# Seven-product block method, first layer: sums of products continued in a PSUM bank, and some late sums moved from GpSimd to VectorE

## The chip, the cores and the metric

The kernel runs on one core of one Trainium2 chip. TensorE (PE in the profile) multiplies, with separate weight loads (PEld); VectorE (DVE), ScalarE (ACT) and GpSimd (POOL) work on elements; SyncE (SP) issues the transfers. The metric is the device time of one execution in microseconds (us). Everything is fp32 where this text is concerned.

## The reference

The program is an attention in which a query sees only keys of its own cluster, followed by a two-layer network with the activation h / (1 + exp(-1.702 h)).

```python
mask = q_assign[:, :, :, None] == k_assign[:, :, None, :]
scores = np.where(mask, scale * q @ k.T, -1e9)      # (4, 8, 768, 768)
x = (softmax(scores) @ v)                            # -> (3072, 512)
h = x @ w_in                                         # (512, 2048)
g = h * (1.0 / (1.0 + np.exp(-1.702 * h)))
return (g @ w_out).astype(np.float32)                # (2048, 512)
```

Four batches (b) of 768 tokens each go through it.

## The kernel before, in words

**Stages.** The attention of all four batches comes first. Batch 0's result stays in SBUF, that of batches 1 to 3 is stored to DRAM (`kept`, L580) and loaded again later. While the attention runs, VectorE also rounds the weights `w_in` and `w_out`. Then, batch by batch, come the first layer (`first7`, L847, once for each f from 0 to 7) and the second layer (`second49`, L890, once for each k from 0 to 6). The order of instructions on every engine is the order in which the Python code calls them; nothing is rescheduled.

**First layer.** A batch's x is cut into 2 x 2 blocks: X[c, h] has 256 of the 512 channels (half c) and 384 tokens (half h). `A_in(row, col, f)` is a piece of `w_in`: 128 outputs, piece f of half `row`, and channel half `col`. The four results of a turn f are `g1[:, 0]`, `g1[:, 1]` (output half 0, token halves 0 and 1) and `g2[:, 0]`, `g2[:, 1]` (output half 1), which are parts of the tile `G`. A plain product of 2 x 2 blocks takes eight block products; the kernel uses a block method with seven, whose operands are also sums of blocks: T1 to T4, sums of X blocks (`sums_x`, VectorE), and S1 to S4, sums of weight blocks (`sums_w`, L610, GpSimd, two turns ahead, in two rotating tiles `W`; S3 is made in place in `w_in`, in batch 0 only). Each block product is two matmul calls (two chunks of 128 channels) into one PSUM bank, and each call shows as two PE records. Seven products are A11·X, S2·T2, S1·T1, S3·T3, S4·X, A22·T4 and A12·X, in this order. Before, each takes a bank of its own out of six (`ps_b`), and VectorE puts them together in `G` with seven additions (`add`, L845); ScalarE copies the first product (L864) and applies the activation in place to the four results (`finish`, L859).

**After the first layer's turns.** `after7(f)` (L883) subtracts in `G` on VectorE, and from f = 4 on makes the first operands of the second layer (`sums_t`). In batch 0 the turns also carry the preparation of `w_out`: `sums_z` (turns 0 to 2, on GpSimd for every third f and on VectorE for the others), `turn_w` (turns 3 and 4, VectorE), and `keep_w` (turns 3 to 6, GpSimd: three sums, and a store of each to `kept_w` by SyncE).

**Second layer.** The same method on two levels: 7 x 7 = 49 products for each batch, seven in each call of `second49`. Already before, these go on in a bank with `start=False` while ScalarE copies the states. Its operands `temps(k)` (tiles E, Tx, Y, parts of G) are made by VectorE while the previous k runs (`extra`, L1087); its weights `Wz` are loaded from `kept_w`, except that in batch 0 the ones for k = 5 and 6 are made on the spot (`load_sums(k, made=True)`, L790). After each k the outer sums over `Y` run on GpSimd, in the last batch on VectorE for the blocks 5 and 7 (L941). In k = 5 and 6 VectorE also makes the next batch's T1 to T4.

**Memory reuse.** `att.close()` (L716) gives the attention's SBUF and PSUM back, and `G` lies there; the first instruction that writes `G`, ScalarE's copy of the first product of batch 0, therefore waits for everything that still used it, among others GpSimd and the stores of `kept`.

Of the kernel before, what the change touches and what calls it, by code (L numbers as in the profile page):

```python
# [8 lines left out]
FP32 = mybir.dt.float32  # L9
# [4 lines left out]
AF = mybir.ActivationFunctionType  # L14
# [24 lines left out]
def fast(  # L39
# [26 lines left out]
    nc = tc.nc  # L66

    B, H, S, D = q.shape
    NC = centroids.shape[1]
    DM, DF = moe_w_in.shape  # L70
    P = 128
    NJ = S // P
    HALF = S // 2
# [231 lines left out]
    for a in range(2):  # L305
        rows = slice(a * D, (a + 1) * D)
        nc.vector.tensor_copy(
            out=cT[rows, :, a, :],
# [287 lines left out]
    def sums(engine, todo):  # L596
        for o, a, op, b in todo:
            engine.tensor_tensor(out=o, in0=a, in1=b, op=(  # L598
                ALU.add if op == "+" else ALU.subtract))
# [3 lines left out]
    def A_in(row, col, f):  # L603

        at = (row * FB + f) * P
        return w_in[:, 2 * col:2 * col + 2, at:at + P]
# [164 lines left out]
        a = W_of(i)  # L771
        sums(nc.vector, ((a(0, 1), a(0, 0), "-", a(0, 1)),))

    def keep_w(k, o):

        a = W_of(ORDER[k])
        s2, s1, s4 = o
        for i, (o, x, op, z) in enumerate((
                (s2, a(1, 1), "-", a(0, 1)), (s1, s2, "+", a(0, 0)),
                (s4, a(1, 0), "-", s2))):  # L780
            sums(nc.gpsimd, ((o, x, op, z),))
            nc.sync.dma_start(out=kept_w[k, i], in_=o)

    def spare_y():
# [3 lines left out]
    W = {}  # L788

    def load_sums(k, made=False):  # L790
        W[k] = ws.tile([P, 3, FQ, P], FP32, name="Wz")
        if made:
            keep_w(k, [W[k][:, i] for i in range(3)])
            return
        for i in range(3):
            nc.sync.dma_start(out=W[k][:, i], in_=kept_w[k, i])
# [47 lines left out]
    def add(o, p, a):  # L844
        nc.vector.tensor_tensor(out=o, in0=p, in1=a, op=ALU.add)  # L845

    def first7(b, f, X, T):  # L847

        S = w_of.pop(b * FB + f)

        def product(a, x):
            ps = ps_b.tile([P, 512], FP32, name="b")
            for c in range(2):
                nc.tensor.matmul(out=ps[:, 0:HALF], lhsT=a[:, c], rhs=x(c),  # L854
                                 start=(c == 0), stop=(c == 1))
            return ps[:, 0:HALF]

        def finish(g):
            nc.scalar.activation(out=g, in_=g, func=AF.Gelu_apprx_sigmoid,  # L859
                                 scale=2.0)  # L860

        g1, g2 = G[:, f], G[:, f + FB]
        p = product(A_in(0, 0, f), lambda c: X[0, 0, c])
        nc.scalar.copy(g1[:, 0], p)  # L864
        p = product(S[2], lambda c: T[2, c])
        add(g2[:, 1], p, g1[:, 0])
        p = product(S[1], lambda c: T[1, c])
        add(g1[:, 1], p, g2[:, 1])
        p = product(S[3], lambda c: T[3, c])
        add(g2[:, 0], p, g2[:, 1])  # L870
        add(g2[:, 1], p, g1[:, 1])
        p = product(S[4], lambda c: X[1, 1, c])
        add(g1[:, 1], p, g1[:, 1])
        finish(g2[:, 1])
        p = product(A_in(1, 1, f), lambda c: T[4, c])
        add(g2[:, 0], p, g2[:, 0])
        finish(g1[:, 1])
        p = product(A_in(0, 1, f), lambda c: X[1, 0, c])
        add(g1[:, 0], p, g1[:, 0])
        finish(g2[:, 0])  # L880
        finish(g1[:, 0])

    def after7(f):  # L883

# [5 lines left out]
    def second49(k, extra, last):  # L890

        i = ORDER[k]
        a, g, t, w = W_of(i), G_of(i), temps(k), W.pop(k)
        A = {1: a(0, 0), 2: a(1, 0), 3: w[:, 2], 4: a(1, 1), 5: w[:, 1],
             6: w[:, 0], 7: a(0, 1)}
        M = {1: g(0, 0), 2: g(1, 0), 3: g(1, 1), 4: t[4], 5: t[1], 6: t[2],
             7: t[3]}

        def bank_b():
            return ps_b.tile([P, 512], FP32, name="b")[:, 0:QT]  # L900

        def product(ps, n, start):
            for f in range(FQ):
                nc.tensor.matmul(out=ps, lhsT=A[n][:, f], rhs=M[n][:, f],  # L904
                                 start=start and f == 0,
                                 stop=(f == FQ - 1), skip_group_check=True)

        y = Y[22] if i == 1 else ep.tile([P, 2, HALF], FP32, name="y")
        y11, y12, y21, y22 = (y[:, m, q * QT:(q + 1) * QT]
                              for m in range(2) for q in range(2))  # L910
        p5 = ep.tile([P, QT], FP32, name="p5")
        x = bank_b()
        product(x, 1, True)
        nc.scalar.copy(y11, x)
        z = bank_b()
        product(z, 2, True)
        add(y11, z, y11)
        extra(0)
        product(x, 6, False)
        nc.scalar.copy(y12, x)  # L920
        v = bank_b()
        product(v, 5, True)
        nc.scalar.copy(p5, v)
        product(x, 7, False)
        nc.scalar.copy(y22, x)
        add(y22, y22, p5)
        extra(1)
        product(v, 3, False)
        add(y12, v, y12)
        if i == 4:  # L930
            c = Y[21]
            add(c[:, 0], y[:, 0], c[:, 0])
            add(c[:, 1, QT:], y22, c[:, 1, QT:])
            extra(2)
        product(x, 4, False)
        if i == 4:
            add(c[:, 1, 0:QT], x, c[:, 1, 0:QT])
            return
        nc.scalar.copy(y21, x)
        extra(2)  # L940
        pool = nc.vector if last and i in (5, 7) else nc.gpsimd  # L941
        sums(pool, {1: (),
                    2: ((Y[11], y, "+", Y[22]),),
                    3: ((Y[12], y, "+", Y[22]),),
                    6: ((Y[12], y, "+", Y[12]), (Y[21], y, "+", Y[22])),
                    5: ((Y[12], y, "+", Y[12]), (Y[22], y, "+", Y[21])),
                    7: ((Y[22], y, "+", Y[22]), (Y[21], y, "+", Y[21]))}[i])
# [80 lines left out]
    for b in range(B):  # L1028
        for f in range(FB):
            first7(b, f, *XT)  # L1030
            sums_w(b * FB + f + 2)
            if f:
                after7(f - 1)
            do(pend, 1)
            if b == 0 and f < 3:
                for n in range(3 * f, min(3 * f + 3, FB)):
                    sums_z((nc.gpsimd, nc.vector, nc.vector)[n % 3], n)
            if b == 0 and f in (3, 4):
                for i in ORDER[0:4] if f == 3 else ORDER[4:]:
                    turn_w(i)  # L1040
            if b == 0 and f >= 3:
                for k in {3: (0,), 4: (1, 2), 5: (3,), 6: (4,), 7: ()}[f]:
                    keep_w(k, spare_y())
                if 5 <= f < 7:
                    load_sums(f - 5)
        after7(FB - 1)
        if b < B - 1:
            for h in range(2):
                for hp in range(HP):
                    x = xT_of[b + 1, h, hp] = xp.tile([P, HALF], FP32,  # L1050
                                                      name="x")
                    nc.sync.dma_start(out=x, in_=kept[b, h, hp])
            made = sums_x(b + 1)
        else:
            made = iter(())

        def stores(b, *todo, **how):
            for n in todo:
                store(b, n, **how)
                yield  # L1060

        def tail():
            store(b, 22)
            yield

        def chain(*todo):
            for steps in todo:
                yield from steps

        def sums_of_x():  # L1070
            for XT[:] in made:
                yield

        x_steps = sums_of_x()
        final = b == B - 1

        for k in range(7):
            nxt = sums_t(k + 1) if k < 6 else iter(())
            more = {1: sums_G(6), 2: sums_G(5), 3: sums_G(4),
                    4: stores(b, 11), 5: stores(b, 12) if final else x_steps,  # L1080
                    6: tail() if final else x_steps}.get(k, iter(()))
            if b == B - 1 and k < 2:
                test(k)
            if (b, k) == (B - 1, 6):
                is_bad = nc.values_load(bad[0:1, 0:1], min_val=0, max_val=1)

            def extra(at):  # L1087
                do(nxt, (2, 1, 1)[at])
                do(more, ((1, 0, 1) if final else (0, 4, 4))[at] if k == 6
                   else (0, 0, 4)[at] if k == 2 else (0, 2, 2)[at])  # L1090

            second49(k, extra, final)
            if k < 5:
                load_sums(k + 2, b == 0 and k > 2)
            elif b < B - 1:
                load_sums(k - 5)
        pend = () if final else stores(b, 12, 22, 21)
        if final:
            store_last(b)
# [439 lines left out]
```

## Time and profile before

| | us |
|---|---|
| median of 3 runs (lowest, highest) | 898.75 (898.56, 899.88) |
| the profiled execution: its time, its span | 900.34, 898.5 |
| PE busy | 885.8 (99%) |
| DVE busy | 728.3 (81%) |
| ACT busy | 366.1 (41%) |
| POOL busy | 497.4 (55%) |
| batch 0: first layer begins, second layer begins | 342.05, 414.33 |
| batch 1: first layer begins, second layer begins | 480.68, 554.83 |
| batch 2: first layer begins, second layer begins | 618.79, 691.03 |
| batch 3: first layer begins, second layer begins | 754.99, 827.23 |

The span runs from the first to the last instruction. Idle time before a group of instructions is put down to the releaser that came last. A line number such as L598 or L845 is that of a helper (`sums`, `add`), so the tile names tell the place. TensorE's granted clock was 0.999 of full speed.

### The profile page before, as it was taken

To read this page: it belongs to the slowest core of one execution; us is meant where nothing else is said; L and a number is where in the kernel's file an instruction comes from. 1 tells how busy PE (TensorE), PEld (TensorE's weight loads), DVE (VectorE), ACT (ScalarE), POOL (GpSimd) and SP (SyncE) were. 2 spreads that over 40 slices of the span, in tenths; PEclk is the share of its full clock that TensorE was granted. 3 is DMA by queue.
4 is the path that set the end of the run, shared out by engine and by line. 5 is a ranking of instruction groups with operands and counts; after the bars stand their busy time and mean duration, and the time that the engine had idled before them with its cause. 6 is when DMAs were issued, how large, how long until landed. Compare 5 with 4: busy or idle time off the path is not lost.

```text
span 898.5 us, 17781 instructions
## 1 busy us (share of the span) xinstructions
PE 885.8 (99%) x6720; PEld 581.4 (65%) x6720; DVE 728.3 (81%) x1183; ACT 366.1 (41%) x819; POOL 497.4 (55%) x469
## 2 busy tenths in 40 slices
PE   8999999999999999999999999999999999999997
PEld 3444444444444445558996557998556998556996
DVE  4999989999999997998998556798556798556795
ACT  3677767777677764322111232111232111222111
POOL 5899999998999998693274221143121134120130
PEclk9999999999999999999999999999999999999999
DMA  9566556666575310036113202223202223200224
GB/s 175 122 129 112 103 120 130 143 143 133 133 139 119 85 43 19 0 122 230 71 54 107 52 1 71 84 74 107 53 1 70 73 76 117 43 10 0 71 71 109
DMA packets 176333, 78.97 MB, mean 88 GB/s; under 512 B 152824, under 2 KB 159472, under 8 KB 176240
## 3 DMA queue, kind: packets, MB, share of 16 engines
q1 hardware_dynamic: 175984, 77.63, 35.2%
q8 instruction: 55, 0.90, 0.4%
q14 instruction: 38, 0.31, 0.1%
q10 hardware_dynamic: 256, 0.13, 0.1%
HBM read 61.03 MB, written 16.70 MB: 87 GB/s over the span
## 4 chain that ended last, share of the span: by engine, by line
PE 87%; DVE 8%; issue 2%; POOL 1%; DMA 1%; ACT 0%; SPq 0%; DVEq 0%; ACTq 0%; POOLq 0%
PE b L854 32%; PE b L904 23%; PE s L472 13%; PE o L537 12%; PE s L495 3%; PE m L554 3%; DVE G L598 2%; DVE E L598 2%; POOL sum L521 1%; PE m L348 1%; DVE Tx L598 1%; DMA in<-in_k_dram 1%; DVE x L598 0%; DVE e L200 0%; DVE y L845 0%
## 5 line engine op out<-in xcount | busy, mean ns | idle before, releaser
L521 POOL TENSOR_TENSOR sum<-sum,A 128x384 f32<-128x384 f32 x252 | 265.5, 1091 | 25.7 <-ACT A L503 16.6
L845 DVE TENSOR_TENSOR G<-b,G 128x384 f32<-128x384 f32 x224 | 123.1, 556 | 98.7 <-PE b L854 89.5
L503 ACT ACTIVATE A<-s 128x768 f32<-128x768 f32 x192 | 146.3, 809 | 91.1 <-PE s L495 71.0
L598 POOL TENSOR_TENSOR Y<-y,Y 128x768 f32<-128x768 f32 x28 | 67.4, 2421 | 175.0 <-DVE y L845 151.0
L859 ACT ACTIVATE G<-G 128x384 f32<-128x384 f32 x128 | 66.3, 523 | 199.1 <-DVE G L845 197.7
L472 PE MATMUL s<-T,T 64*64 64x384 f32 x1536 | 142.9, 487 | 0.7 <-ACT A L503 0.7
L537 PE MATMUL o<-A,inv 64*64 64x384 f32 x1536 | 141.2, 483 | 0.0
L598 POOL TENSOR_TENSOR W<-w_in 128x256 f32<-128x256 f32 x32 | 23.6, 737 | 163.8 <-PE b L854 163.5
L598 DVE TENSOR_TENSOR G<-G 128x768 f32<-128x768 f32 (+1 forms) x92 | 104.5, 1159 | 0.0
L472 PEld LDWEIGHTS s<-T,T 64*64 64x64 f32 x1536 | 54.9, 132 | 70.1 <-ACT A L503 36.4
L854 PE MATMUL b<-x,W 128*128 128x384 f32 x256 | 93.1, 486 | 0.0
L854 PE MATMUL b<-Tx,w_in 128*128 128x384 f32 x256 | 93.1, 486 | 0.0
L854 PE MATMUL b<-x,w_in 128*128 128x384 f32 x256 | 88.6, 486 | 0.0
L537 PEld LDWEIGHTS o<-A,inv 64*64 64x64 f32 x1536 | 58.3, 133 | 38.5 <-issue 33.5
L854 PEld LDWEIGHTS b<-x,W 128*128 128x128 f32 x256 | 48.6, 190 | 33.9
L854 PEld LDWEIGHTS b<-Tx,w_in 128*128 128x128 f32 x256 | 48.6, 190 | 33.9
L854 PEld LDWEIGHTS b<-x,w_in 128*128 128x128 f32 x256 | 48.5, 190 | 33.5 <-issue 0.6
L904 PE MATMUL b<-G,w_out 128*128 128x192 f32 x320 | 55.9, 326 | 0.0
L904 PEld LDWEIGHTS b<-G,w_out 128*128 128x128 f32 x320 | 52.7, 190 | 1.1
L904 PE MATMUL b<-E,Wz 128*128 128x192 f32 x288 | 51.5, 328 | 1.4 <-DVE E L598 1.4
L904 PEld LDWEIGHTS b<-E,Wz 128*128 128x128 f32 x288 | 47.1, 190 | 3.4 <-POOL Wz L598 1.3
L854 PE MATMUL b<-Tx,W 128*128 128x384 f32 x128 | 46.6, 487 | 1.5 <-DVE Tx L598 1.5
(169 smaller groups left out, 1366.4 us busy)
## 6 DMA issues: line engine op xcount, KB each, us to landing
Wz<-kept_w SPq DMA_DIRECT2D x78, 256.0 KB
raw<-in_moe_w_in_dram SPq DMA_DIRECT2D x16, 512.0 KB
raw<-in_moe_w_out_dram SPq DMA_DIRECT2D x16, 512.0 KB
inv<-in_v_dram SPq DMA_DIRECT2D x16, 384.0 KB
in<-in_q_dram SPq DMA_DIRECT2D x60, 96.0 KB
in<-in_k_dram SPq DMA_DIRECT2D x60, 96.0 KB
kept<-x SPq DMA_DIRECT2D x24, 192.0 KB
x<-kept SPq DMA_DIRECT2D x24, 192.0 KB
```

Source lines behind the costliest of these rows:

```text
L348: nc.tensor.matmul(out=ps[r:r + SQ, w * NJ * SQ:(w + 1) * NJ * SQ] .rearrange("p (j t) -> p j t", t=SQ), lhsT=cT[:, p % HP].rearrange("p a ...
L472: nc.tensor.matmul(out=ps[c:c + D, a, 0:HALF], lhsT=T[p, 1][rows, kt * P + c:kt * P + c + D], rhs=T[p, 0][rows, h * HALF:(h + 1) * HALF], ...
L495: nc.tensor.matmul(out=s_of[u][c:c + D, a, :], lhsT=rows_of[1, p % 2][rows, kt * P + c:kt * P + c + D], rhs=rows_of[0, p % 2][rows, h * HA ...
L503: nc.scalar.activation(out=A_of[u], in_=s_of.pop(u), func=AF.Exp, scale=SCALE)
L521: nc.gpsimd.tensor_tensor(out=sum_of[g][:, a], in0=(A_of[u - 1] if kt == 1 else sum_of[g])[:, a], in1=A_of[u][:, a], op=ALU.add)
L537: nc.tensor.matmul(out=o_of[g][a * D:(a + 1) * D, r, 0:HALF], lhsT=v_in[p][rows, a, kt, :], rhs=A[rows, a, :], start=(kt == 0), stop=(kt = ...
L554: nc.tensor.matmul(out=ps[a * D:(a + 1) * D, 0:HALF], lhsT=twos, rhs=sm[:, a, :], start=(i == 0), stop=(i == len(parts) - 1))
L598: engine.tensor_tensor(out=o, in0=a, in1=b, op=(ALU.add if op == "+" else ALU.subtract))
L845: nc.vector.tensor_tensor(out=o, in0=p, in1=a, op=ALU.add)
L854: nc.tensor.matmul(out=ps[:, 0:HALF], lhsT=a[:, c], rhs=x(c), start=(c == 0), stop=(c == 1))
L859: nc.scalar.activation(out=g, in_=g, func=AF.Gelu_apprx_sigmoid, scale=2.0)
L904: nc.tensor.matmul(out=ps, lhsT=A[n][:, f], rhs=M[n][:, f], start=start and f == 0, stop=(f == FQ - 1), skip_group_check=True)
```

## The change

In `first7` three banks x, z and v are taken in each turn, in place of seven. The order of the products becomes A11·X into x, A12·X into z, S2·T2 on top of x, S1·T1 into v, S3·T3 on top of x, S4·X on top of v, A22·T4 on top of x. ScalarE copies x after its first and its second product, and v after its first; VectorE does three additions; the last activation reads x from PSUM. In batch 0 the sums of `keep_w` for k = 5 and 6 and the outer sums of blocks 5 and 7 go from GpSimd to VectorE.

```diff
-    def keep_w(k, o):
+    def keep_w(k, o, engine=nc.gpsimd):
...
-            sums(nc.gpsimd, ((o, x, op, z),))
+            sums(engine, ((o, x, op, z),))
             nc.sync.dma_start(out=kept_w[k, i], in_=o)
...
         if made:
-            keep_w(k, [W[k][:, i] for i in range(3)])
+            keep_w(k, [W[k][:, i] for i in range(3)], nc.vector)
             return
...
-        def product(a, x):
-            ps = ps_b.tile([P, 512], FP32, name="b")
+        def product(ps, a, x, start=True):
             for c in range(2):
-                nc.tensor.matmul(out=ps[:, 0:HALF], lhsT=a[:, c], rhs=x(c),
-                                 start=(c == 0), stop=(c == 1))
-            return ps[:, 0:HALF]
-
-        def finish(g):
-            nc.scalar.activation(out=g, in_=g, func=AF.Gelu_apprx_sigmoid,
-                                 scale=2.0)
+                nc.tensor.matmul(out=ps, lhsT=a[:, c], rhs=x(c),
+                                 start=start and c == 0, stop=(c == 1),
+                                 skip_group_check=True)
+
+        def bank_b():
+            return ps_b.tile([P, 512], FP32, name="b")[:, 0:HALF]
+
+        def finish(g, ps=None):
+            nc.scalar.activation(out=g, in_=g if ps is None else ps,
+                                 func=AF.Gelu_apprx_sigmoid, scale=2.0)
 
         g1, g2 = G[:, f], G[:, f + FB]
-        p = product(A_in(0, 0, f), lambda c: X[0, 0, c])
-        nc.scalar.copy(g1[:, 0], p)
-        p = product(S[2], lambda c: T[2, c])
-        add(g2[:, 1], p, g1[:, 0])
-        p = product(S[1], lambda c: T[1, c])
-        add(g1[:, 1], p, g2[:, 1])
-        p = product(S[3], lambda c: T[3, c])
-        add(g2[:, 0], p, g2[:, 1])
-        add(g2[:, 1], p, g1[:, 1])
-        p = product(S[4], lambda c: X[1, 1, c])
-        add(g1[:, 1], p, g1[:, 1])
+        x, z, v = (bank_b() for _ in range(3))
+        product(x, A_in(0, 0, f), lambda c: X[0, 0, c])
+        nc.scalar.copy(g1[:, 0], x)
+        product(z, A_in(0, 1, f), lambda c: X[1, 0, c])
+        add(g1[:, 0], z, g1[:, 0])
+        product(x, S[2], lambda c: T[2, c], False)
+        nc.scalar.copy(g1[:, 1], x)
+        finish(g1[:, 0])
+        product(v, S[1], lambda c: T[1, c])
+        nc.scalar.copy(g2[:, 1], v)
+        product(x, S[3], lambda c: T[3, c], False)
+        add(g2[:, 1], x, g2[:, 1])
         finish(g2[:, 1])
-        p = product(A_in(1, 1, f), lambda c: T[4, c])
-        add(g2[:, 0], p, g2[:, 0])
+        product(v, S[4], lambda c: X[1, 1, c], False)
+        add(g1[:, 1], v, g1[:, 1])
         finish(g1[:, 1])
-        p = product(A_in(0, 1, f), lambda c: X[1, 0, c])
-        add(g1[:, 0], p, g1[:, 0])
-        finish(g2[:, 0])
-        finish(g1[:, 0])
+        product(x, A_in(1, 1, f), lambda c: T[4, c], False)
+        finish(g2[:, 0], x)
...
-            second49(k, extra, final)
+            second49(k, extra, b in (0, B - 1))
```

## The prediction, made before the changed kernel was run

> **What bounds the kernel now.** I read the page's busy times first (PE 99%), then the stages of the feed-forward part, then the time lines of single engines where a stage is longer than its matmuls. Stages (us, busy us and instruction count of each engine, clock, DMA):
>
> ```profile
> 342.05:414.33 72.28, 72.28 (x226) 42.60 (x226) 65.56 (x101) 21.14 (x45) 59.02 (x64) 1.00 0.22 76
> 414.33:460.16 45.83, 45.77 (x282) 45.47 (x280) 40.18 (x54) 9.04 (x27) 11.93 (x6) 1.00 0.26 92
> 460.16:480.68 20.52, 19.13 (x114) 18.09 (x114) 20.45 (x19) 3.19 (x10) 16.73 (x9) 1.00 0.40 136
> 480.68:554.83 74.15, 72.66 (x226) 42.63 (x226) 44.35 (x86) 20.04 (x39) 18.62 (x25) 1.00 0.16 43
> ```
>
> A first-layer product takes 1.29 us (four records of 0.3225), a turn of seven 9.03, eight turns 72.24; batches 2 and 3 take just that. A second-layer product takes 1.30, 49 take 63.7; batches 1 and 2 take 63.96. So TensorE sets the end, and only where it waits is there something to gain. Batch 0 takes 66.35 for its second layer, and batch 1 74.15 for its first. Where, PE's time line of batch 0 tells (start, us, operation, idle before):
>
> ```profile
> 462.87 1.54 PE L904 MATMUL b<-Tx,Wz 128*128 128x192 f32 x8
> 465.08 1.54 PE L904 MATMUL b<-E,Wz 128*128 128x192 f32 x8 [0.67 <-DVE E L598]
> 475.40 1.54 PE L904 MATMUL b<-E,Wz 128*128 128x192 f32 x8 [0.68 <-DVE E L598]
> 480.68 1.45 PE L854 MATMUL b<-x,w_in 128*128 128x384 f32 x4
> 483.62 1.56 PE L854 MATMUL b<-Tx,W 128*128 128x384 f32 x4 [1.49 <-DVE Tx L598]
> ```
>
> k = 5 runs from 460.16 to 470.35 (10.19, against 9.10), k = 6 to 480.68 (10.33), and batch 1's second product comes 2.94 after its first instead of 1.29, the third 1.39 after that. Together 1.09 + 1.23 + 1.65 + 0.10 = 4.07 us, all waits for VectorE. VectorE is busy for 20.45 of the 20.52 us there, because its sums are stretched by GpSimd's: the one at 469.51 takes 2.45 us, a like one elsewhere 0.95. The same in batch 0's first layer:
>
> ```profile
> 351.79 0.41 DVE L598 TENSOR_TENSOR w_out<-w_out 128x256 f32<-128x256 f32 x1
> 352.24 0.83 DVE L598 TENSOR_TENSOR Z<-w_out 128x256 f32<-128x256 f32 x1
> 353.11 0.83 DVE L598 TENSOR_TENSOR Z<-Z,w_out 128x256 f32<-128x256 f32 x1
> 353.86 0.95 DVE L598 TENSOR_TENSOR Z<-w_out,Z 128x256 f32<-128x256 f32 x1
> 354.74 0.94 DVE L598 TENSOR_TENSOR w_out<-w_out 128x256 f32<-128x256 f32 x1
> 355.72 0.43 DVE L598 TENSOR_TENSOR Z<-w_out 128x256 f32<-128x256 f32 x1
> ```
>
> GpSimd has sums until 355.4; while it does, a VectorE sum takes about 0.85, afterwards 0.43. TensorE doesn't feel this today: with six banks it runs up to five products (6.45 us) ahead of VectorE. The start of batch 0 shows that slack, on ScalarE's time line:
>
> ```profile
> 347.29 0.48 ACT L864 COPY G<-b 128x384 f32<-128x384 f32 x1 [2.19 <-POOL W L598]
> 347.78 1.28 ACT L859 ACT_TABLE_LOAD   x1
> 350.10 1.65 ACT L859 ACTIVATE G<-G 128x384 f32<-128x384 f32 x3 [1.04 <-DVE G L845]
> 352.61 0.48 ACT L864 COPY G<-b 128x384 f32<-128x384 f32 x1 [0.17 <-PE b L854]
> ```
>
> The first product starts at 342.05 and is done at 343.34, yet its copy starts at 347.29, since G's memory is not free before (put down to GpSimd; the store of kept issued at 345.1 fits as well). Six products fit in meanwhile.
>
> **What the Trainium skill says.** SBUF — State Buffer, "Who interferes with whom": a VectorE instruction with two SBUF inputs and a GpSimd one that reads SBUF exclude each other for the whole instruction; one with a PSUM operand doesn't take part. The trace agrees: 0.83 against 0.43 above, and L845's additions from PSUM (mean 556 ns) are not stretched. PSUM — Partial Sum Buffer, "The four PSUM rules": a synchronised read in the middle of an accumulation group is allowed; the second layer does it at 326 ns a record, full rate. ScalarE: Activation LUTs, "What ACT_TABLE_LOAD costs": 1.28 us plus 1.38 of drain; the trace shows the 1.28, and at most 2.32 from its start to the activation behind it. TensorE: Matmul & The Clock Gate, "What's actually happening": an idle window of about 3.4 us halves the clock; no pause so long stands in this trace after the start.
>
> **The change part by part.** TensorE's products are the same in number and size: 0. VectorE loses four of seven additions a turn (4 x 0.53 = 2.1 us), ScalarE gains two copies (2 x 0.48); both are hidden behind 9.03 us of matmuls. What counts is the new order of waits: x and v must be read before TensorE goes on in them, one product (1.29 us) later.
>
> Steady turn: a copy starts 1.53 after its product's start (351.08 to 352.61) and takes 0.48; with 0.15 until TensorE goes on (E done at 475.25, matmul at 475.40) that is 2.16, due at 2.58: 0.42 to spare. VectorE's addition on x: 1.40 + 0.56 + 0.15 = 2.11, 0.47 to spare. ScalarE's activation between the copies of x and v ends 5.11 into the turn, v is ready for it at 5.40. So 0 in batches 1 to 3, if VectorE is free; after each turn it has at most 3 us of sums, and its next addition is due at 2.7 without TensorE waiting for it.
>
> (a) Start. The third product, on top of x, is due at 342.05 + 2.58 = 344.63, but the copy ends at 347.77; it starts at 347.92. **+3.29.** Nothing in the change touches what the copy waits for. VectorE and GpSimd's W sums for turn 2, both queued behind these products, move along.
>
> (b) Table load. It stands behind the second copy now: that ends at 347.92 + 2.01 = 349.93, load 1.28, activation 0.52, copy of v 0.48, to TensorE 0.15: 352.36. S4 on v is due at 347.92 + 3.87 = 351.79: **+0.57** (with the drain up to +1.6; I take the trace's).
>
> (c) Turns 1, 2 and 4. ScalarE's queue has the activation of g1[:, 0] ahead of v's copy, and it waits for VectorE's addition of z, which stands behind the previous turn's sums. VectorE starts those at -0.62 (turn start = 0), when the addition on v is done. GpSimd's three W sums come after S4, the sixth product now and not the fifth, at -1.2, and its sum for `sums_z` (four) and S3 (one) behind: eight in all, alongside. Turn 1: eight VectorE sums, seven at 0.85 and one at 0.41, to +5.74; addition 0.56, activation 0.55, copy 0.50, TensorE 0.15: 7.50, due 6.45: +1.05. Turn 2: after7 on top, +1.54. Turn 4: after7 0.5, four `turn_w` of which two at 1.1 beside W sums and two at 1.68 (like 380.55's), to +5.4: +0.65. Turns 3, 5, 6 and 7 have 4 to 5.4 us of sums: about 0. **+3.24**, between 0 (no stretching) and 6 (all at 0.95 and later turns too).
>
> (d) Second half. From 459 on GpSimd has nothing left in batch 0, so VectorE's stretched sums shrink: the excess over 0.95 (0.35, 0.5 for shorter ones) of those between 459.03 and 483 adds up to 12.1 us. VectorE takes over six sums of 128x512 (0.65) and four of 128x768 (0.95): 7.7. Net 4.4 us earlier at the end, and batch 1's T2 is due one product later. Those of k = 5 come some 0.2 us before they are needed. The six stores keep their place in SyncE's queue; nothing urgent is behind them. **-4.07**; bounds -4.07 and 0.
>
> (e) Each second layer's third product waits 0.26 for the last turn's sums (63.96 - 63.7; batch 3 shows it too, from 829.67 to 832.53). The addition on v is one product earlier than the last one now: three times **-0.26** = -0.78.
>
> Sum: 3.29 + 0.57 + 3.24 - 4.07 - 0.78 = +2.25. On the profiled span 898.5 that gives 900.75; that execution took 900.34, 1.6 over the median, so I put the same difference on the median: **901.0 us**.
>
> **Rivals.** *Not slower* (0.20): VectorE's sums get by without meeting GpSimd's, the eight take 3.4 us and (c) is 0: 897.8. For it: VectorE has 15 us less work in this layer. Against: eight sums stand on both engines after the same product. It decides when (c) is under 1.0. *Early copy* (0.08): G is free when the first product is done, so (a) is 0: 897.7; against: its list of waits is unchanged. *A wait in every turn* (0.09): the 0.42 isn't there. If four hand-overs in 32 turns each miss by 0.1, that is 12.8: 914. In this group I count a halved clock after the pause in (a), too, some +1.7. *No gain in (d)* (0.08): VectorE, with 7.7 us more, is late for k = 5 and 6 all the same: 905.1. The likeliest, 0.55, has 899.7 to 903.5 for its own range.
>
> **How the numbers follow.** This kernel's measurement can tell about 0.2% (1.8 us) from nothing. Slower by more: 0.47 of the likeliest, 0.09 and 0.08: 0.64. Within: 0.08 of the likeliest, 0.13 and 0.04: 0.25. Faster: 0.07 + 0.04 = 0.11. The range 898.2 to 905.5 leaves out about a tenth at each end.
>
> **What would show it.** In the changed profile: PE idle about 3.3 us before the third product of batch 0, released by ScalarE's copy; idle of 1 to 1.5 us before S4 in turns 1 and 2, put down to ScalarE; first layers of batches 1 to 3 at 72.24; batch 0's second layer at about 64 and no wait for Tx in batch 1. The prediction is wrong if later turns wait, or if batch 0's first layer is under 76 us.

## The result, and the profile after

| | before | after |
|---|---|---|
| median, us (lowest, highest; 6 runs each) | 899.11 (898.56, 900.03) | 904.32 (903.91, 905.70) |
| ratio of times, 95% interval | | 1.0057 [1.0047, 1.0068] |
| profiled execution: its time, its span | 900.34, 898.5 | 904.76, 903.0 |
| VectorE additions at L845 in that execution | 224, 123.1 us | 96, 53.5 us |
| PE, DVE, ACT, POOL busy | 885.8, 728.3, 366.1, 497.4 | 886.5, 666.3, 393.8, 487.0 |

The changed kernel is slower by 5.2 us. VectorE has 62 us less to do, and the time went up all the same: what counts is TensorE's waits. Here are its waits in the changed kernel, from batch 0's first product to the end of batch 1's first layer (waited for, us in all, number, longest):

```profile
PE b L853 <- ACT G L874: 3.2, 3, 1.5
PE b L853 <- ACT G L867: 3.1, 1, 3.1
```

Before, this stretch had three waits, all for VectorE, 2.9 us in all (those of k = 5, k = 6 and T2). These are gone. In their place stand four for ScalarE: one for its copy of the first product (L867), three for its copy of v (L874). All four lie in one stage. The two halves of batch 0 as windows (us; busy us and count of PE, PEld, DVE, ACT, POOL; clock; DMA share; GB/s):

```profile
341.57:423.05 81.48, 75.13 (x225) 43.05 (x225) 53.35 (x71) 29.54 (x62) 59.05 (x63) 0.98 0.18 65
423.05:487.21 64.16, 64.02 (x394) 63.65 (x393) 58.37 (x84) 11.41 (x36) 11.37 (x6) 1.00 0.35 113
```

The first window has 81.48 us for 72.24 us of matmuls, and a clock of 0.98; the second has what its matmuls need. Stage by stage, from the start of one stage's first matmul to the next's:

| us | batch 0, first | batch 0, second | batch 1, first | second | batch 2, first | second | batch 3, first | second |
|---|---|---|---|---|---|---|---|---|
| before | 72.35 | 66.35 | 73.99 | 63.96 | 72.24 | 63.96 | 72.24 | 64.07 |
| after | 81.48 | 64.16 | 72.24 | 63.78 | 72.24 | 63.77 | 72.29 | 63.81 |

(Batch 0's start is taken at its first record, at 341.98 before and 341.57 after; in every kernel here that product takes 1.40 us, 0.11 more than the others.) The first layer of batch 0 costs 9.13 more, the next two stages give 2.19 and 1.75 back, the rest 0.58. With a start 0.41 earlier that makes +4.20 up to the closing transposes; the spans differ by 4.5.

Where the 9 us are is seen on PE's time line (start, us, operation, tiles, count, idle before and releaser):

```profile
341.57 2.85 PE L853 MATMUL b<-x,w_in 128*128 128x384 f32 x8
347.49 2.90 PE L853 MATMUL b<-Tx,W 128*128 128x384 f32 x4 [3.07 <-ACT G L867]
350.19 1.72 PE L853 MATMUL b<-x,W 128*128 128x384 f32 x4
351.74 1.45 PE L853 MATMUL b<-Tx,w_in 128*128 128x384 f32 x4
353.26 1.53 PE L853 MATMUL b<-x,W 128*128 128x384 f32 x4
...
361.07 1.45 PE L853 MATMUL b<-Tx,w_in 128*128 128x384 f32 x4
363.55 1.53 PE L853 MATMUL b<-x,W 128*128 128x384 f32 x4 [1.02 <-ACT G L874]
...
371.36 1.45 PE L853 MATMUL b<-Tx,w_in 128*128 128x384 f32 x4
374.30 1.53 PE L853 MATMUL b<-x,W 128*128 128x384 f32 x4 [1.48 <-ACT G L874]
```

The starts are what to read: a product should begin 1.29 after the one before. (The idle time shown is 0.16 to 0.18 shorter than the delay, since a record's modelled end runs past the next due start.) The third product is due at 341.57 + 1.40 + 1.29 = 344.26 and starts at 347.49: 3.23 late. (Where an expectation below has 3.34 for this pause, the 0.11 of the first product is in it.) Its four records then take 2.70 instead of 1.29, and the next product's 1.55: 1.67 lost. S4 of turn 0 starts 1.52 after S3, not 1.29: 0.23. S4 of turns 1 and 2 is late by 1.19 and 1.65, that of turn 4 (393.31) by 0.88. Together 8.85; what is left of 9.13 is 0.28, some 0.07 behind each wait.

The four records are long because the clock fell. The same stretch and the next product as windows (columns as above; the clock is the third number from the end):

```profile
347.49:350.19 2.70, 2.70 (x5) 1.49 (x6) 0.45 (x1) 0.00 (x0) 0.19 (x1) 0.50 0.00 0
350.19:351.74 1.55, 1.55 (x5) 0.91 (x4) 0.00 (x0) 1.29 (x2) 0.00 (x0) 0.83 0.00 0
```

Half speed for 2.70 us, right behind a pause of 3.2 us. On ScalarE's time line of the changed kernel the copies that release the products are seen:

```profile
346.87 0.48 ACT L867 COPY G<-b 128x384 f32<-128x384 f32 x1 [2.19 <-POOL W L598]
350.43 0.48 ACT L871 COPY G<-b 128x384 f32<-128x384 f32 x1 [3.08 <-PE b L853]
350.93 1.28 ACT L861 ACT_TABLE_LOAD   x1
352.22 0.52 ACT L861 ACTIVATE G<-G 128x384 f32<-128x384 f32 x1
352.65 0.46 ACT L874 COPY G<-b 128x384 f32<-128x384 f32 x1
...
362.51 0.52 ACT L861 ACTIVATE G<-G 128x384 f32<-128x384 f32 x1 [2.05 <-DVE G L845]
362.94 0.46 ACT L874 COPY G<-b 128x384 f32<-128x384 f32 x1
```

The last two lines are turn 1: the activation of `g1[:, 0]` waits for VectorE's addition of z, and the copy of v that TensorE needs stands behind it. VectorE's line tells why that addition is late. Two of the eight sums ahead of it, and the addition itself:

```profile
357.60 0.95 DVE L598 TENSOR_TENSOR Z<-w_out,Z 128x256 f32<-128x256 f32 x1
...
361.07 0.94 DVE L598 TENSOR_TENSOR Z<-w_out,Z 128x256 f32<-128x256 f32 x1
361.94 0.55 DVE L845 TENSOR_TENSOR G<-b,G 128x384 f32<-128x384 f32 x1
```

All eight are stretched (0.65 to 0.95), the last one too; they end at 362.01, 6.1 us into the turn. In the second half of batch 0 it is the other way round. Two of VectorE's sums for k = 6, which before took 2.30 and 2.45 us while GpSimd had the late sums:

```profile
478.43 0.95 DVE L598 TENSOR_TENSOR G<-G 128x768 f32<-128x768 f32 x1
479.41 0.96 DVE L598 TENSOR_TENSOR E<-G 128x768 f32<-128x768 f32 x1
```

### The profile page after: what moved, and what is told of

Read it like the earlier page. It is cut to its first block, busy times and chain, and to the rows that moved or that the text cites. A ratio compares the mean times of both kernels' runs of the same rounds, so it can differ in the third digit from the quotient of the medians.

```text
span 903.0 us, 17649 instructions
## 1 busy us (share of the span) xinstructions
PE 886.5 (98%) x6720; PEld 584.2 (65%) x6720; DVE 666.3 (74%) x1065; ACT 393.8 (44%) x883; POOL 487.0 (54%) x459
## 4 chain that ended last, share of the span: by engine, by line
PE 92%; DVE 5%; issue 1%; ACT 1%; DMA 1%; SPq 0%; ACTq 0%; DVEq 0%
PE b L853 30%; PE b L905 25%; PE s L472 14%; PE o L537 14%; PE s L495 3%; PE m L554 3%; DVE G L598 2%; PE m L348 1%; DVE Z L598 1%; DVE E L598 1%; DMA in<-in_k_dram 1%; DVE Tx L598 0%; DVE w_out L598 0%; PE o L296 0%; DVE G L845 0%
## 5 line engine op out<-in xcount | busy, mean ns | idle before, releaser
L845 DVE TENSOR_TENSOR G<-b,G 128x384 f32<-128x384 f32 x96 | 53.5, 557 | 163.5 <-PE b L853 158.0
L598 POOL TENSOR_TENSOR Y<-y,Y 128x768 f32<-128x768 f32 x24 | 61.6, 2579 | 161.9 <-DVE y L845 134.7
L598 DVE TENSOR_TENSOR G<-G 128x768 f32<-128x768 f32 (+1 forms) x92 | 102.2, 1135 | 0.0
L861 ACT ACTIVATE G<-G 128x384 f32<-128x384 f32 x96 | 50.4, 525 | 74.2 <-DVE G L845 74.1
```

The source lines that it names most:

```text
L598: engine.tensor_tensor(out=o, in0=a, in1=b, op=(ALU.add if op == "+" else ALU.subtract))
L861: nc.scalar.activation(out=g, in_=g if ps is None else ps, func=AF.Gelu_apprx_sigmoid, scale=2.0)
```

## The experiments

**The moves alone.** The kernel before with nothing but the late sums of batch 0 on VectorE. This asks whether step (d) is the moves' own.

```diff
-    def keep_w(k, o):
+    def keep_w(k, o, engine=nc.gpsimd):
...
-            sums(nc.gpsimd, ((o, x, op, z),))
+            sums(engine, ((o, x, op, z),))
...
-            keep_w(k, [W[k][:, i] for i in range(3)])
+            keep_w(k, [W[k][:, i] for i in range(3)], nc.vector)
...
-            second49(k, extra, final)
+            second49(k, extra, b in (0, B - 1))
```

> The kernel before with only the sums moved from GpSimd to VectorE (keep_w for k = 5 and 6, outer sums of blocks 5 and 7 in batch 0). My theory: the moves give step (d) by themselves, since the waits of k = 5, k = 6 and of batch 1's T2 (1.09 + 1.23 + 1.65 + 0.10 us) came from VectorE being held up by GpSimd: about 4.0 us faster than before, near 895.1, with batch 0's second layer at about 64 us. Rival: the gain seen after the change came from the four additions fewer on VectorE; with all seven back, 7.7 us more work make VectorE late all the same: within 1 us of before or slower.

896.41 us against 900.03, ratio 0.9956 [0.9943, 0.9970]. (The ratios are worked out from all the runs of a set, and differ a little from the quotient of the two medians.) No wait of TensorE is listed from batch 0's first product to the end of batch 1's first layer. Batch 0 and the first layer of batch 1 as windows:

```profile
342.50:414.84 72.34, 72.34 (x226) 42.66 (x225) 65.38 (x101) 21.09 (x45) 58.76 (x64) 1.00 0.21 75
414.84:479.23 64.39, 64.21 (x394) 63.65 (x392) 58.61 (x86) 12.21 (x37) 9.88 (x4) 1.00 0.34 110
479.23:551.47 72.24, 72.24 (x226) 42.56 (x225) 41.62 (x83) 20.01 (x39) 17.13 (x24) 1.00 0.17 44
```

64.39 for 66.35 and 72.24 for 73.99: 3.7 us gained by the moves alone, nearly all of step (d). That rival, no gain in (d), falls.

**The banks alone.** The changed kernel with the late sums left on GpSimd.

```diff
-            keep_w(k, [W[k][:, i] for i in range(3)], nc.vector)
+            keep_w(k, [W[k][:, i] for i in range(3)])
...
-            second49(k, extra, b in (0, B - 1))
+            second49(k, extra, final)
```

> The changed kernel with the sums left on GpSimd. My theory: the waits of k = 5 and k = 6 come back (1.09 + 1.23), that for T2 only in part, since T2 is due one product later (1.65 becomes some 0.5): about 3 us slower than the changed kernel, near 907. Rival (VectorE's lighter first layer alone gives the gain): the same as the changed kernel, 904.3.

906.73 us, ratio 1.0076 [1.0062, 1.0091]. TensorE's waits from batch 0's second layer to the end of batch 1's first:

```profile
PE b L905 <- DVE E L598: 0.7, 1, 0.7
PE b L853 <- DVE Tx L598: 0.3, 1, 0.3
```

A sum of VectorE's in k = 6 is as long as before the change:

```profile
476.44 2.45 DVE L598 TENSOR_TENSOR E<-G 128x768 f32<-128x768 f32 x1
```

Yet the wait in k = 5 didn't come back, and that for T2 is 0.29 instead of 1.49, as T2 is wanted one product later in the new order. The two stages take 65.03 and 73.10, so only 1.7 us is lost against the changed kernel, between what the theory and its rival had asked for. So with the banks in place the moves are worth 1.7; without them, 3.7. The two parts of the change overlap in (d): each alone removes some of the same waits. Why the wait in k = 5 stays away without the moves was not tried by itself.

**Activation behind the copy.** ScalarE's activation of `g1[:, 0]` goes behind its copy of v, in all turns.

```diff
         nc.scalar.copy(g1[:, 1], x)
-        finish(g1[:, 0])
         product(v, S[1], lambda c: T[1, c])
         nc.scalar.copy(g2[:, 1], v)
+        finish(g1[:, 0])
```

> The changed kernel with one pair swapped on ScalarE: the activation of g1[:, 0] stands behind the copy of v, not ahead of it. My theory for turns 1, 2 and 4 (and for the table load in turn 0): TensorE waits for v's copy, which is held up only because ScalarE's queue has this activation, which waits for VectorE, in front. So the waits before S4 (0.23 + 1.19 + 1.65 + 0.88 us) go, about 4 us: near 900.3, with VectorE's sums in turns 1 and 2 as long as before. Rival: VectorE itself is what is late, and the wait only moves one product on, to A22 on top of x, which needs the addition on x: 903 to 904.3.

900.88 us, ratio 1.0006 [0.9997, 1.0014]. Turns 1, 2 and 4 take 9.03 each, and one wait is left in batch 0's first layer. VectorE's sums are as long as ever in turn 1 (0.83 to 0.95 us), so it is the order of ScalarE's queue that turned them into TensorE's waits, and they didn't move on to another product. PE's time line at the start:

```profile
346.88 2.90 PE L853 MATMUL b<-Tx,W 128*128 128x384 f32 x4 [3.09 <-ACT G L867]
349.57 2.77 PE L853 MATMUL b<-x,W 128*128 128x384 f32 x4
352.13 1.87 PE L853 MATMUL b<-Tx,w_in 128*128 128x384 f32 x4
353.84 1.45 PE L853 MATMUL b<-x,W 128*128 128x384 f32 x4
```

The layer takes 78.68: 72.35 as before, the pause of 3.24, and 3.1 of slow clock. Here two products and part of a third are slow; in the changed kernel it was one and a little.

**Filling the pause.** Twelve bf16 matmuls of 512 columns into a spare bank, between batch 0's second and third product.

```diff
+        if b == 0 and f == 0:
+            spare = bank()
+            for _ in range(12):
+                nc.tensor.matmul(
+                    out=spare, lhsT=ident_h,
+                    rhs=ident_h[:, None, :].broadcast_to((P, 4, P)),
+                    start=True, stop=True)
         product(x, S[2], lambda c: T[2, c], False)
```

> The changed kernel with twelve bf16 matmuls of 128x512 on constants into a spare bank put ahead of the third product of batch 0, where TensorE pauses for 3.3 us; they do nothing for the result and end within the pause. Theory: the four records behind the pause took 2.70 us instead of 1.29, and those of the next product 1.55, because TensorE's clock fell in the pause. With the pause filled they run at 0.3225 us a record: about 1.6 us faster than the changed kernel, near 902.7, the third product at the same time. Rival: they were slow for another reason (weights of W, hand-over of the bank): 904.3, the records as slow as before.

904.08 us, ratio 1.0036 [1.0022, 1.0050], an interval that overlaps the changed kernel's [1.0047, 1.0068] a little, so the times by themselves don't settle the gain. PE's time line:

```profile
345.12 2.75 PE L873 MATMUL m<-ident_h 128*128 128x512 bf16 x12
348.37 1.53 PE L853 MATMUL b<-Tx,W 128*128 128x384 f32 x4 [0.50 <-ACT G L867]
349.74 1.45 PE L853 MATMUL b<-x,W 128*128 128x384 f32 x4
...
352.76 1.53 PE L853 MATMUL b<-x,W 128*128 128x384 f32 x4 [0.28 <-ACT G L881]
```

The third product starts 5.94 after the first, as in the changed kernel (5.92), but it and the next run at full rate. The layer takes 80.12, 1.36 less. TensorE's mean clock over an execution agrees: 0.998 or 0.999 in all five here, 0.996 or 0.997 in five of the changed kernel's six (0.999 in the other). So the slow products were the pause's doing; the delay itself is another matter. With faster products the wait for the table load grows, from 0.23 to 0.44.

**Turn 0 of batch 0 as before.** Only this one turn of the 32 has seven banks and seven additions; the rest is the changed kernel.

```diff
-            first7(b, f, *XT)
+            (first7_old if b == 0 and f == 0 else first7)(b, f, *XT)
```

> The changed kernel, but turn 0 of batch 0 alone in the form of before (seven banks, seven additions). Theory for step (a): TensorE's pause comes from the first write into G, which is late, being wanted one product after the first; with seven banks in this one turn nothing waits for it. So the pause (3.34 us), the slow records behind it (1.67) and the table load's wait (0.23) go, 5.2 us: ratio to before near 1.000, batch 0's first layer at about 76.2 us, with the waits of turns 1, 2 and 4 as they were. Rival: VectorE, which then begins its sums while GpSimd is still behind, is later in turn 1, and half of it comes back: 1.003.

899.56 us, ratio 0.9992 [0.9983, 1.0000]. The pause, the slow clock and the table load's wait are gone, the layer takes 76.19, and the three waits for the copy of v remain. The copy of the first product, at 347.44, is even later (6.25 after the first product's start, 5.30 in the changed kernel), and stops nobody: the other products of the turn have banks of their own. The longest of the three waits, in turn 2 (the others are 0.88 and 0.70):

```profile
368.63 1.53 PE L853 MATMUL b<-x,W 128*128 128x384 f32 x4 [1.48 <-ACT G L874]
```

**What the first copy waits for.** GpSimd's sums for turn 1, three W sums and one in `w_in`, are called after the attention's memory is given back, and not before it.

```diff
         if t == NT - 1:
             sums_w(0)
-            sums_w(1)
...
+    sums_w(1)
     for b in range(B):
```

> The changed kernel with the weight sums of turn 1 on GpSimd issued after the attention's memory is given back, not before; GpSimd's own order is the same. It tells what the first copy into G waits for. If it is GpSimd's sums (theory: all it had been given by then), the copy starts some 2 us earlier, near 345, TensorE's pause falls from 3.3 to about 1.2 us and its clock stays: 3.5 us faster than the changed kernel, ratio to before near 1.002. Rival: it is the store of kept issued at about 345, which lands near 346.9: then nothing moves, ratio 1.0057.

905.04 us, ratio 1.0053 [1.0038, 1.0069]: no gain. The copy on ScalarE's line, and the last store of `kept` on SyncE's:

```profile
346.88 0.48 ACT L866 COPY G<-b 128x384 f32<-128x384 f32 x1 [2.21 <-POOL W L598]
```

```profile
344.73 0.32 SPq L580 DMA_DIRECT2D kept<-x  x1
```

GpSimd's sums that come before the release were done at 343.70, and the copy still started at 346.88. The releaser that the profile names is hardly the cause, since GpSimd's sums after 343.70 are called behind the release and end at 346.99, after the copy's start. What remains is the store, issued at 344.73, 2.15 ahead of the copy, with data moving until about 346.2. That it is the store was not tried by itself, but the other executions speak for it. In three of them the store's data took longer, and the copy came later by as much, while GpSimd's sums did not: they end 2.25 to 2.27 behind the store's issue in all four (us):

| | store issued | its last data | GpSimd's three W sums end | copy starts |
|---|---|---|---|---|
| changed kernel | 344.73 | 346.2 | 346.99 | 346.87 |
| the moves alone | 345.66 | 347.4 | 347.91 | 348.19 |
| turn 0 as before | 344.35 | 346.7 | 346.62 | 347.44 |
| both mends | 342.96 | 345.3 | 345.22 | 346.09 |

In all eleven executions the copy starts 0.6 to 0.8 behind the store's last data; against the W sums it lies anywhere from 0.1 before their end to 0.9 after it.

TensorE's pause, 3.24, is as long as in the changed kernel, but in this execution the clock stayed up:

```profile
347.50 1.53 PE L852 MATMUL b<-Tx,W 128*128 128x384 f32 x4 [3.08 <-ACT G L866]
```

The same pause, and no slow product behind it.

**When the clock falls.** The traces of all the kernels show what decides. In each of them the time from one change of the clock to the next is a whole multiple of 3.413 us, as if it were decided anew at the edges of stretches of that length. In the changed kernel's trace it is full for 337.92 us (99 times 3.413), half for 3.413, and full again for 549.55 (161 times 3.413). The stretch with most of the pause in it, and the next one, in the changed kernel and in this one (TensorE's busy time is the second number, the clock the third from the end):

```profile
343.89:347.30 3.41, 0.53 (x2) 0.00 (x0) 0.78 (x2) 1.22 (x4) 3.25 (x5) 1.00 0.15 58
347.30:350.71 3.41, 3.22 (x5) 1.85 (x6) 0.56 (x1) 0.33 (x2) 0.38 (x1) 0.50 0.00 0
```

```profile
345.65:349.06 3.41, 1.56 (x5) 1.06 (x6) 0.56 (x1) 0.48 (x1) 2.03 (x3) 1.00 0.13 49
349.06:352.47 3.41, 3.13 (x10) 1.62 (x9) 0.56 (x1) 2.75 (x5) 0.00 (x0) 1.00 0.00 0
```

The same for all the kernels with a pause or a filled pause here:

| | stretch | TensorE busy in it | clock in the next stretch |
|---|---|---|---|
| changed kernel | 343.89 to 347.30 | 0.53 | 0.50 |
| GpSimd without its sums | 343.38 to 346.79 | 0.65 | 0.50 |
| activation behind the copy | 342.73 to 346.14 | 1.07 | 0.50, and again in the one after it |
| banks alone | 345.23 to 348.64 | 1.39 | 0.50 |
| GpSimd's turn-1 sums later | 345.65 to 349.06 | 1.56 | 1.00 |
| S1·T1 first | 344.80 to 348.21 | 1.71 | 1.00 |
| pause filled | 345.54 to 348.96 | 2.92 | 1.00 |

So it is not the length of the pause alone: a stretch with 1.39 us of work or less was followed by half speed, one at full speed with 1.56 or more was not. (The limit is not sharper than that here: right at the start of the execution with GpSimd's turn-1 sums later, a stretch with 1.58 us of work was followed by half speed too. And a stretch that was slow itself, behind the pause of the activation behind the copy, stayed slow with 2.67 us of work; those with 3.11 or more were followed by full speed.) With GpSimd's turn-1 sums later, the edge of two stretches cut the pause in parts of 1.2 and 1.9, and both kept enough work. In the banks alone the slow stretch began at 348.64, behind the third product, and it was the fourth and fifth that were slow. An estimate from these numbers: 3.07 us of idle time escape only if both parts are under some 1.85 to 2.02 (3.41 less 1.56, and less 1.39), which is so for a fifth to a quarter of the places where the edge can fall; 1.8 us or less escape everywhere. A slow stretch costs at most 1.7 (half of 3.41).

**GpSimd without its sums for w_out.** In batch 0's first turns GpSimd writes zeros in place of its sums in `sums_z`; this part of the computation is left out.

```diff
-                    sums_z((nc.gpsimd, nc.vector, nc.vector)[n % 3], n)
+                    if n % 3:
+                        sums_z(nc.vector, n)
+                    else:
+                        for i in (1, 2, 4):
+                            nc.gpsimd.memset(Sz(i, n), 0.0)
```

> The changed kernel with GpSimd's four sums of sums_z in turns 0, 1 and 2 replaced by three writes of zeros to the same tiles, which read nothing (the weights of the second layer are wrong by it, so its result too). Theory for step (c): VectorE's eight sums in turns 1 and 2 are long because they exclude each other with GpSimd's one for one; those beside the zeros run at 0.43 us, only those beside the W sums and S3 (four) at about 0.85. VectorE is done about 1.7 us earlier, and TensorE's waits of 1.19 and 1.65 us before S4 in turns 1 and 2 go or nearly; that of turn 4 stays. Rival: VectorE's sums are long for their own operands (two tiles read and written in place): they stay at 0.83 to 0.95, and so do the waits.

901.46 us in one run. The waits in turns 1 and 2 are gone, that of turn 4 (no zeros there) is still 0.70, and the layer takes 78.48. VectorE's line in turn 1, and GpSimd's beside it:

```profile
357.19 0.41 DVE L598 TENSOR_TENSOR Z<-w_out,Z 128x256 f32<-128x256 f32 x1
357.53 0.41 DVE L598 TENSOR_TENSOR w_out<-w_out 128x256 f32<-128x256 f32 x1
357.98 0.83 DVE L598 TENSOR_TENSOR Z<-w_out 128x256 f32<-128x256 f32 x1
```

```profile
356.93 0.81 POOL L1042 MEMSET Z<- 128x256 f32 x3
357.71 0.81 POOL L598 TENSOR_TENSOR w_in<-w_in 128x256 f32<-128x256 f32 x1
```

Beside GpSimd's zeros, which read nothing, a sum takes 0.41; as soon as GpSimd adds again (357.71), VectorE's next one takes 0.83. The stretching is GpSimd's reading sums, as step (c) said.

**Both mends.** The changed kernel with turn 0 of batch 0 as before and the activation behind the copy of v, that is, the two edits shown above together. If the two causes are separate and complete, the layer should be back at about 72.3.

> The changed kernel with both repairs: turn 0 of batch 0 in the form of before, and in all other turns the activation of g1[:, 0] behind the copy of v. If the theory holds, all of steps (a), (b) and (c) is gone and (d) and (e) stay: batch 0's first layer near 72.4 us, its second near 64.1, the later second layers 63.78; 4.8 us faster than before, ratio near 0.9947, and faster than the moves alone (0.9956) by 0.6 to 0.9 us. Rival: a wait behind them shows up, such as for the addition on x before A22 in turns 1 and 2: ratio 0.997.

895.63 us, ratio 0.9953 [0.9942, 0.9965]: faster than both kernels. The two halves of batch 0:

```profile
339.79:412.25 72.46, 72.46 (x226) 42.58 (x226) 53.28 (x75) 28.61 (x60) 58.66 (x63) 1.00 0.20 71
412.25:476.39 64.14, 64.01 (x394) 63.64 (x392) 58.35 (x84) 11.38 (x36) 11.35 (x6) 1.00 0.35 115
```

No wait of TensorE is listed in this stretch, and the later stages take 72.24 to 72.29 and 63.77 to 63.78. The layer has 72.46, for 81.48 in the changed kernel. From the first product to the closing transposes it is 544.73 us, against 549.16 before and 545.44 with the moves alone. So the banks are worth 0.7 us by the traces once their waits are mended; in the runs' times that can't be told from the moves alone (0.9956).

**S1·T1 first.** In turn 0 of batch 0, v's first product goes ahead of the one on top of x, so that TensorE has three products and not two before it needs the late copy.

```diff
         add(g1[:, 0], z, g1[:, 0])
+        early = b == 0 and f == 0
+        if early:
+            product(v, S[1], lambda c: T[1, c])
         product(x, S[2], lambda c: T[2, c], False)
...
-        product(v, S[1], lambda c: T[1, c])
+        if not early:
+            product(v, S[1], lambda c: T[1, c])
```

> The changed kernel, but in turn 0 of batch 0 alone TensorE makes S1·T1 into v ahead of S2·T2 on top of x: one more product that waits for no copy. Theory: the first write into G stays where it is, so the product on top of x starts at the same time, about 5.9 us after the first, and TensorE's pause there falls from 3.34 to about 2.05 us; if a pause has to be some 3 us long to lower the clock, the records behind it run at full rate (1.29 us for four) in every execution. About 2.5 us faster than the changed kernel, ratio to before near 1.003, batch 0's first layer near 78.7 us. Rival (any pause of 2 us lowers the clock too): 1.29 us faster at most, four records of 2.7 us again.

903.60 us, ratio 1.0038 [1.0022, 1.0053]. PE's line:

```profile
347.06 1.56 PE L853 MATMUL b<-Tx,W 128*128 128x384 f32 x4 [1.70 <-ACT G L867]
349.19 1.56 PE L853 MATMUL b<-Tx,w_in 128*128 128x384 f32 x4 [0.57 <-ACT G L874]
351.48 1.53 PE L853 MATMUL b<-x,W 128*128 128x384 f32 x4 [0.74 <-ACT G L878]
```

The pause is down to 1.70 of idle time and no product behind it is slow, as expected. But two waits came in: S3, now straight behind S2 in the same bank, waits for the copy in between (0.84 late), and S4 waits for the table load, the activation and the copy of v (1.0 late). The layer takes 80.05, 1.4 less than in the changed kernel where the shorter pause (1.86 for 3.23) and the clock gave back 3.0. A hand-over that had a product to hide under lost it.

## Why the prediction was right in sign and short in size

The direction, the places of the waits and the whole range (898.2 to 905.5) held. The forecast was 901.0, the median is 904.32: 0.8 above what the likeliest group of the prediction allowed (899.7 to 903.5), because the mechanism of that group came together with a term that was left to a rival. By terms, from the profiled executions (us):

| step | predicted | measured |
|---|---|---|
| (a) third product waits for the first copy | +3.29 | +3.23 |
| clock behind that pause | 0 (put under a rival, at +1.7) | +1.67 |
| (b) table load | +0.57 | +0.23 |
| (c) turns 1, 2, 4 | +1.05, +1.54, +0.65 | +1.19, +1.65, +0.88 |
| small losses behind these waits | 0 | +0.28 |
| (d) second half of batch 0, start of batch 1 | -4.07 | -2.19 - 1.75 = -3.94 |
| (e) later stages | -0.78 | -0.58 |
| start of batch 0 | 0 | -0.41 |
| sum | +2.25 | +4.20 |

**The step that failed is the clock behind (a):** put at 0 in the sum, measured at 1.67. The prediction knew of it: it had worked out a pause of 3.3 us and quoted an idle window of about 3.4 from the Trainium skill (TensorE: Matmul & The Clock Gate, "What's actually happening"). It took 3.3 for short enough and left the halving to a rival of small chance. The page also says that the window runs freely, and that when the clock changes depends on where the work falls in it; the traces agree, with stretches of 3.41 us. But the window need not be idle as a whole: up to 1.39 us of work in it were followed by half speed, and there the measurement decides. The banks alone, the activation behind the copy, GpSimd without its sums and the changed kernel lost 1.6 to 3.1 us to slow products; the kernel with GpSimd's turn-1 sums moved lost nothing. Four of five lose, as the estimate above would have it, so the halving belonged into the sum as the likelier case. That the pause is the cause is shown by filling it and by the table of stretches. That the range held owes something to luck: two slow stretches in place of one, as with the activation behind the copy, would have added some 1.4 (3.1 for 1.67) and put the median at about 905.7, above the range (an estimate).

**(c) had the right mechanism and was 0.48 short.** The eighth sum was taken at 0.41 and was stretched too, since GpSimd was still adding. That the stretched sums are one half of the cause and ScalarE's order the other is shown from both sides: zeros on GpSimd take away the waits of turns 1 and 2, the swap takes away all three. The rival that VectorE gets by without meeting GpSimd falls.

**(a) held to 0.06, whatever releases the copy.** The prediction left GpSimd and the store of `kept` side by side; that GpSimd's turn-1 sums are not what counts was shown by moving them, and in all eleven executions the copy follows the store's last data.

**(b) was 0.34 too dear here** in part because of the slow products: S4 was due 0.26 later, as the product ahead of S3 took 1.55 and not 1.29. Where the clock stayed up, the wait was 0.44 (pause filled) and 0.45 (GpSimd's turn-1 sums moved). It used the trace's load time without the 1.38 us of drain that the Trainium skill gives (ScalarE: Activation LUTs, "What ACT_TABLE_LOAD costs"). That choice was right: the load starts 0.02 after the copy ahead of it ends, and the activation starts at 352.22, 0.01 after the load's end at 352.21.

**(d) and (e) held,** within 0.13 and 0.20. The reason given for (d), less overlap with GpSimd, is confirmed by the moves alone; the prediction named T2's later due time, but didn't see that the new order in PSUM by itself removes about half of the same waits.

**Steady turns cost nothing,** as worked out from 0.42 us of slack: batches 1 to 3 take 72.24 to 72.29. A wait in every turn falls. The forecast missed the median by 3.32. The terms above make 1.95 of it and the stretch behind the closing transposes 0.3. The rest is in how the profiled executions stand to the medians: before's was 1.59 above the median that the forecast was set on, after's only 0.44 above its own.

## What to carry to other kernels

Going on in a PSUM bank with a copy in between saves elementwise work, but turns a slack of five products into a deadline one product later; look first at the turn where the reader is late for another reason (memory that is reused, a table load), and leave that turn with banks of its own. On the engine that reads the bank, put the copy that TensorE needs ahead of everything that waits for a third engine. Reckon a TensorE pause of some 3 us with the slow products that can follow it, even where one execution shows none; in the two layers, waits of up to 1.70 us of idle time brought none in any trace here.

## What the runs showed of the hardware that was not expected

- The clock changed at whole multiples of 3.413 us, and a stretch of that length need not be idle to bring half speed: it followed stretches with 0.53 to 1.39 us of TensorE work, and not those with 1.56 to 2.92 around the pause. So pauses of the same 3.2 us cost 1.7 in one kernel, 3.1 in another and nothing in a third.
- The slow products need not stand right behind the pause: in the banks alone the first product behind it ran at full rate, and the two after it were slow.
- The activation behind a table load began 0.01 us after it.
- The releaser named for the first copy of batch 0 misleads: moving GpSimd's sums behind the release changed neither the name nor the wait (2.19 and 2.21 us), and the copy followed the store's last data by 0.6 to 0.8 us in every execution.
